# Six buffers instead of five for the splits of a Down phase, those splits ranked ahead of the weights' splits, and B22 loaded before B21

## The chip, the cores and the metric

One core of one Trainium2 chip runs the whole kernel. The metric is the device time of one execution in microseconds (us). The engines are named as the profile names them: PE (matmuls), PEld (its weight loads), ACT, DVE, POOL, and SP, which here issues nearly all DMAs.

## The reference, cut to what matters

```python
x = attention(q, k, v, omega)            # linear attention, 2304 tokens x 512
h = x @ w_in;  h = h * sigmoid(h)        # 512 -> 2048      "up 1"
x = h @ w_out                            # 2048 -> 512      "down 1"
g = x @ w_gate; v = x @ w_val            # 512 -> 1536      "up 2"
return (g * sigmoid(g) * v) @ w_out2     # 1536 -> 512      "down 2"
```

The weights come as float64 and are brought to float32 on the chip ("conv" in the code). All matrices are multiplied in float32 accuracy.

## The kernel before, in words

Five stages follow each other on PE: attention (0 to about 118 us), up 1 (to 292), down 1 (to 469), up 2 (to 722), down 2 (to the end).

Each matrix product of the four later stages is a Strassen scheme with seven products in place of eight, in the order `ORDER` = 1, 5, 6, 2, 7, 3, 4 (P1, P5, P6, P2, P7, P3, P4 below). Every product takes one block of the weights and one block of the tokens: B11 for P1, T1 = B12 - B11 for P5, T2 = B22 - T1 for P6, B21 for P2, T3 = B22 - B12 for P7, B22 for P3, T4 = B21 - T2 for P4. Each operand is split into a high part ("hi", a copy on ACT in the reduced format fp32r) and the rest ("lo", a subtraction on DVE), and three matmuls (hi hi, hi lo, lo hi) replace one.

A Down phase (`down_phase`) walks over three groups of 768 tokens (s = 0, 1, 2), in each over the seven products, and in each product over the pairs k of feature blocks: four pairs in down 1, three in down 2. One pair is 12 matmuls (line L1478). For each pair `split` makes the hi (ACT, L1337), the lo (DVE, L1341) and, in P1, P5, P6 and P2, one of T1 to T4 (DVE, L1361). Hi and lo take one buffer each from the free list `f_z`, and give both back when the pair's matmuls are done. The blocks B11, B12, B21, B22 come from DRAM (`zload`, L1311); B22 and B21 land in space that the weights of the up phase used until its last product. The weights of the Down phase are loaded (SP, L1282) and split (ACT L1286, DVE L1290) by `split_load`; three such groups belong to each product of down 1 (widths 768, 768, 512), two to each of down 2. The post-processing of a Down product is L1419 (ACT) and L1433 (DVE); that of an up product is L1120 and L1144 (ACT) and L1177 and L1161 (DVE).

What is put on which engine's queue, and when, is settled when the program is written, by a list scheduler: `streams` holds the waiting operations by kind ("z" the loads of the blocks, "wd" the weights of the Down phase, "split" the hi, lo and T operations, "x" the preparation of the next up phase, "conv" the conversion of weights). `flush` emits, ahead of each product, what would be ready by the scheduler's own clock; the earliest goes first, and of two that are close the stream that stands earlier in the table (0.1 us for each place). On the chip each engine then runs its queue in that fixed order. `hook1` is called ahead of every product of up 1 with the step n (24 steps) and the product p, and opens streams and buffers at fixed places: `open_z` takes two of the six weight buffers of the up phase and gives four of 768 columns to `f_z`. A fifth buffer `gap` of `f_z` lies between B21 and B22 and is given when the Down phase starts; it is taken away again for the last group of tokens, where the weights of up 2 are to be loaded over it.

Of the kernel before, what the change touches and what calls it, by code (L numbers as in the profile page):

```python
# [42 lines left out]
def kernel(  # L43
# [151 lines left out]
    class Stream:  # L195
# [31 lines left out]
    streams = {  # L227
        "z": Stream(0.2),
        "wd": Stream(1.0),
        "split": Stream(1.0),  # L230
        "x": Stream(1.2, DVE=3),
# [87 lines left out]
    W = {}  # L319

    def conv_job(kind, i, dram=None, side=False):
        b = {}
# [17 lines left out]
        def first(h):  # L340
            def go():
                b["c", h] = c = f_c.take()

                nc.scalar.activation(c, word(h, 1).bitcast(F32), AF.Prelu, scale=2.0**-112, alpha=-(2.0**32))  # L349

            return Op("ACT", cost("ACT", 512), go, ins=[key("r", h)], outs=[key("c", h)], slots=(f_c, 1))

# [967 lines left out]

    def down_phase(m, Wd, hook, gap_until=None):
        fp = FP[m]
        np_ = fp // 2
        K = lambda *k: ("d", m, *k)
        gap = cut(ra, 3072, 768)
        ops = {}
# [54 lines left out]
        yield st  # L1381
        f_z.give(gap)
        gone = []

# [71 lines left out]
        for s in range(NSB):  # L1456
            for p in ORDER:
                for k in range(np_):
# [28 lines left out]
                    for t in (hi, lo):  # L1487
                        n = len(lent)
                        lent[:] = [x for x in lent if x is not t]
                        if len(lent) < n:  # L1490
                            f_op.give(t)
                        elif t is not gap or (s, p) != gap_until and not gone:
                            f_z.give(t)
                        else:
                            gone.append(t)
                    if (s, p, k) == (*(gap_until or (0, 0)), np_ - 1) and not gone:
                        f_z.q = deque(x for x in f_z.q if x[0] is not gap)
                        gone.append(gap)
                    if s == NSB - 1 and (k == np_ - 1):
# [4 lines left out]
                ended(s, p)  # L1504
        f_z.q = deque((x, t) for x, t in f_z.q if x is not gap)

# [36 lines left out]
    Wd1, wd_ops = down_ops(0)  # L1543
    d1 = down_phase(0, Wd1, lambda *a: hook_d1(*a), (NSB - 1, 6))

# [3 lines left out]
    def open_z():  # L1549
# [4 lines left out]
        for i in range(4):  # L1554
            f_z.give(cut(ra, 7424 + i * 768, 768))

# [11 lines left out]
    def hook1(n, p):  # L1568
# [5 lines left out]
        if n == len(seq1) - 6 and p == 1:  # L1574
            streams["wd"].extend(wd_ops)
        if n == len(seq1) - 1 and p == 1:
            open_z()
# [7 lines left out]
    assert not to_come  # L1585
    streams["z"].extend(z_first(0, "B21", "B22"))

# [57 lines left out]
    while len(streams["conv"]):  # L1645
        assert drain()
    streams["z"].extend(z_first(1, "B21", "B22"))
    open_z()
# [50 lines left out]
```

## Time and profile before

| | |
|---|---|
| median of 3 runs | 852.97 us (851.78 to 855.28) |
| the profiled execution's own time | 853.52 us |
| its span in the trace | 851.7 us |
| granted PE clock, mean over the span | 0.998 of full |
| PE busy | 823.9 us of the span |

The profiled execution has 1.8 us outside its span, and stands 0.55 us above the median. PE's busy time counts the modelled end of a matmul: after a wait, the first matmul of a new run starts some 0.2 us later than the row's idle figure says, so losses below are counted from start to start. A matmul of a full run takes 0.162 us from start to start (24 of them span 4.06 us with the last one's end of 0.33 us), so a pair of 12 takes 1.94 us.

### The profile page before, as it was taken

Reading aid. Unit: us, or ns where it says so; the run is one execution under the profiler, and the core shown is the slowest. Engines: PE = TensorE matmul, PEld = TensorE weight load, DVE = VectorE, ACT = ScalarE, POOL = GpSimd, SP = SyncE. Lnnn points to the kernel's source line nnn. Section 1 sums busy time; section 2 is a strip of 40 time slices with the busy share of each in tenths; the row PEclk is TensorE's granted clock in tenths of the full one; section 3 lists DMA queues with packets and bytes.
Section 4 is the critical chain, followed back from the end, with each engine's and each line's share of the span. In section 5 each row is a group of like instructions: output and inputs, shape, how many; then the busy total and the mean of one; then the engine's idle time right before and its main releaser. Section 6 shows DMA issues by size and latency. Waiting matters only on the chain.

```text
span 851.7 us, 18196 instructions
## 1 busy us (share of the span) xinstructions
PE 823.9 (97%) x6889; PEld 796.4 (93%) x6889; DVE 623.8 (73%) x1016; ACT 552.5 (65%) x1166; POOL 164.8 (19%) x204
## 2 busy tenths in 40 slices
PE   8999999999999879999998998999999999999998
PEld 7888889999899879999998998999999999899998
DVE  4888877576644687796899998584757548979783
ACT  6999878776767854455557874655556557646552
POOL 0477831044440000000000035121213010000000
PEclk9999999999999999999999999999999999999999
DMA  8579866588999865608514657462637168483602
GB/s 284 183 259 299 282 211 226 173 260 282 333 310 364 286 231 165 206 22 243 181 62 141 218 179 208 146 204 100 211 97 238 53 212 283 169 272 94 220 3 75
DMA packets 110120, 170.09 MB, mean 200 GB/s; under 512 B 9424, under 2 KB 94032, under 8 KB 110032
## 3 DMA queue, kind: packets, MB, share of 16 engines
q1 hardware_dynamic: 109808, 168.69, 60.9%
q8 instruction: 54, 0.88, 0.4%
q14 instruction: 34, 0.28, 0.1%
q10 hardware_dynamic: 224, 0.23, 0.1%
HBM read 107.02 MB, written 61.87 MB: 198 GB/s over the span
## 4 chain that ended last, share of the span: by engine, by line
PE 76%; DVE 7%; DMA 7%; issue 4%; ACT 3%; POOL 2%; SPq 0%; DVEq 0%; ACTq 0%; POOLq 0%
PE ps L1103 36%; PE ps L1478 29%; PE ps L757 4%; PE ps L801 2%; PE ps L817 2%; DMA wd_out<-fa 2%; PE ps L848 2%; DMA ra<-g_d 2%; POOL fa L382 2%; DVE fa L363 1%; DMA fa<-in_moe_w_val 1%; DVE ra L1341 1%; DMA fa<-in_moe_w_out 1%; DVE ra L429 1%; PE ps L873 1%
## 5 line engine op out<-in xcount | busy, mean ns | idle before, releaser
L382 POOL TENSOR_TENSOR fa<-fa 128x256 f32<-128x256 f32 x124 | 105.6, 866 | 506.4 <-ACT fa L1144 239.3
L1103 PE MATMUL ps<-ra 128*128 128x384 f32 x840 | 148.4, 328 | 6.1 <-ACT ps L1120 4.0
L1103 PE MATMUL ps<-rb,ra 128*128 128x384 f32 x840 | 146.3, 327 | 2.1 <-ACT ps L1120 2.1
L1103 PE MATMUL ps<-rc,ra 128*128 128x384 f32 x840 | 145.8, 326 | 1.5 <-ACT ps L1120 1.5
L1103 PEld LDWEIGHTS ps<-ra 128*128 128x128 f32 x840 | 137.6, 189 | 9.0 <-ACT ps L1120 5.8
L1103 PEld LDWEIGHTS ps<-rb,ra 128*128 128x128 f32 x840 | 137.6, 189 | 3.6 <-ACT ps L1120 3.3
L1103 PEld LDWEIGHTS ps<-rc,ra 128*128 128x128 f32 x840 | 137.8, 189 | 2.5 <-ACT ps L1120 2.4
L1120 ACT ACTIVATE ps<-ps 128x384 f32<-128x384 f32 x180 | 85.4, 477 | 67.7 <-PE ps L1103 63.4
L1177 DVE TENSOR_TENSOR fa<-fa,ps 128x384 f32<-128x384 f32 x120 | 66.2, 551 | 80.5 <-ACT ps L1120 58.0
L1337 ACT ACTIVATE ra<-fa 128x768 fp32r<-128x768 f32 x86 | 71.9, 841 | 60.4 <-PE ps L1478 43.9
L1341 DVE TENSOR_TENSOR ra<-fa,ra 128x768 fp32r<-128x768 f32 x81 | 77.4, 955 | 21.6 <-PE ps L1478 13.4
L1478 PE MATMUL ps<-ra 128*128 128x384 f32 x486 | 84.0, 332 | 6.8 <-DVE ra L1341 5.7
L1478 PE MATMUL ps<-ra,rb 128*128 128x384 f32 x516 | 89.9, 327 | 0.4 <-DVE ra L1341 0.4
L1478 PEld LDWEIGHTS ps<-ra 128*128 128x128 f32 x486 | 80.7, 192 | 9.0 <-DVE ra L1341 7.4
L1478 PE MATMUL ps<-ra,rc 128*128 128x384 f32 x482 | 83.9, 327 | 2.2 <-DVE ra L1341 2.2
L1478 PEld LDWEIGHTS ps<-ra,rb 128*128 128x128 f32 x516 | 84.5, 189 | 1.4 <-DVE ra L1341 1.0
L773 ACT ACTIVATE kq<-ps,nb 128x128 f32<-128x128 f32 x288 | 79.3, 401 | 7.8 <-DVE nb L771 7.5
L1478 PEld LDWEIGHTS ps<-ra,rc 128*128 128x128 f32 x482 | 78.9, 189 | 3.4 <-DVE ra L1341 3.2
L349 ACT ACTIVATE fa<-fa 128x512 f32<-128x512 f32 x65 | 54.0, 833 | 20.2 <-DMA fa<-in_moe_w_in 5.7
L1361 DVE TENSOR_TENSOR fa<-ra,fa 128x768 f32<-128x768 f32 x63 | 60.0, 953 | 4.4 <-DMA ra<-g_d 3.7
L1144 ACT ACTIVATE fa<-fa 128x384 f32<-128x384 f32 x84 | 43.6, 519 | 25.5 <-DVE fa L1177 25.2
L363 DVE SCALAR_TENSOR_TENSOR fa<-fa 128x512 uint32<-128x512 uint32 x65 | 56.0, 862 | 0.7
(112 smaller groups left out, 1104.5 us busy)
## 6 DMA issues: line engine op xcount, KB each, us to landing
g_d<-fa SPq DMA_DIRECT2D x168, 192.0 KB, 4.1
fa<-g_d SPq DMA_DIRECT2D x42, 384.0 KB, 5.0
ra<-g_d SPq DMA_DIRECT2D x42, 384.0 KB, 4.3
fa<-in_moe_w_out SPq DMA_DIRECT2D x28, 512.0 KB, 5.1
fa<-in_moe_w_in SPq DMA_DIRECT2D x16, 512.0 KB, 5.0
wd_out<-fa SPq DMA_DIRECT2D x12, 512.0 KB, 3.2
fa<-in_moe_w_gate SPq DMA_DIRECT2D x12, 512.0 KB, 4.0
fa<-in_moe_w_val SPq DMA_DIRECT2D x12, 512.0 KB, 5.2
```

Of the source, the lines that this page charges most:

```text
L349: nc.scalar.activation(c, word(h, 1).bitcast(F32), AF.Prelu, scale=2.0**-112, alpha=-(2.0**32))
L363: nc.vector.scalar_tensor_tensor(c, word(h, 0), 29, c, op0=ALU.logical_shift_right, op1=ALU.bitwise_or)
L382: f(blk(f"S{n}"), blk(l), blk(r))
L773: nc.scalar.activation(e[:, g // 2, g % 2, h * M : (h + 1) * M], x[:, g, :], AF.Exp, bias=nb[:, g : g + 1])
L1103: nc.tensor.matmul(woven(ps[b][:, :N]), cut(l, j * P, P), halves(cut(r, j * N, N)), start=start and c == 0, stop=stop and c == 5, skip_gro ...
L1120: nc.scalar.activation(out() if callable(out) else out, src, AF.Copy)
L1144: nc.scalar.activation(b["t"], src, AF.Silu)
L1177: nc.vector.tensor_add(t, t if in_place else p5[n], ps[bank_][:, :N])
L1337: nc.scalar.activation(ops[s, p, k][0], src(), AF.Copy)
L1341: nc.vector.tensor_sub(l, src(), h.bitcast(F32))
L1361: (nc.gpsimd if eng == "POOL" else nc.vector).tensor_sub(z(PLACE[to]), z(PLACE.get(l, l)), z(PLACE.get(r, r)))
L1478: nc.tensor.matmul(woven(ps[BANKS[p] + e][:, :N]), cut(a, e * P, P), halves(b), start=p in FIRST and i == 0 and c == 0, stop=p in LAST and ...
```

## The change

Nothing is added to or taken from what is computed. The diff, with the parts that only count buffers left out:

```diff
     streams = {
         "z": Stream(0.2),
+        "split": Stream(1.0),
         "wd": Stream(1.0),
-        "split": Stream(1.0),
...
+    halved = []
...
         def first(h):
             def go():
                 b["c", h] = c = f_c.take()
+                halved[:] = [x for x in halved if x is not b] + ([b] if h == 0 else [])
...
-            return Op("ACT", cost("ACT", 512), go, ins=[key("r", h)], outs=[key("c", h)], slots=(f_c, 1))
+            return Op("ACT", cost("ACT", 512), go, ins=[key("r", h)], outs=[key("c", h)], slots=(f_c, 1), guard=lambda: h == 1 or not halved)
...
-        gap = cut(ra, 3072, 768)
+        spares = [cut(ra, 3072, 768), cut(ra, 6912, 768)]
...
-        f_z.give(gap)
-        gone = []
+        for t in spares:
+            f_z.give(t)
+        over = []
...
-                    if (s, p, k) == (*(gap_until or (0, 0)), np_ - 1) and not gone:
-                        f_z.q = deque(x for x in f_z.q if x[0] is not gap)
-                        gone.append(gap)
+                    for t, x in zip(spares, until or ()):
+                        if (s, p, k) == (*x, 0):
+                            over.append(t)
+                            f_z.q = deque(y for y in f_z.q if y[0] is not t)
...
-    d1 = down_phase(0, Wd1, lambda *a: hook_d1(*a), (NSB - 1, 6))
+    d1 = down_phase(0, Wd1, lambda *a: hook_d1(*a), ((NSB - 1, 2), (NSB - 1, 3)))
...
-            f_z.give(cut(ra, 7424 + i * 768, 768))
+            f_z.give(cut(ra, 7680 + i * 768, 768))
...
-        if n == len(seq1) - 1 and p == 1:
+        if n == len(seq1) - 2 and p == 5:
             open_z()
...
-    streams["z"].extend(z_first(0, "B21", "B22"))
+    streams["z"].extend(z_first(0, "B22", "B21"))
...
-    streams["z"].extend(z_first(1, "B21", "B22"))
+    streams["z"].extend(z_first(1, "B22", "B21"))
```

In the changed program the lines of interest stand three further down: L1337, L1341, L1361 are L1340, L1344, L1364; L1286, L1290, L1282 are L1289, L1293, L1285; L1311 is L1314, L1177 is L1180, L1129 is L1132, L586 is L589, L1433 is L1440. PE's matmuls come in the same order as before, but for the buffers that they read. POOL's queue is the same.

**DVE at the start of down 1.** `fa<-fa,ps` is the last post-processing of up 1, `rb<-rb` and `rc<-rc` are lo parts of weights, `ra<-fa,ra` is a pair's lo, `fa<-fa` is T1 and `fa<-ra,fa` is T2 or T3. Before:

```order
L1177 TENSOR_TENSOR fa<-fa,ps_83 128x384
L1290 TENSOR_TENSOR rb<-rb 128x768
L1341 TENSOR_TENSOR ra<-fa,ra 128x768
L1361 TENSOR_TENSOR fa<-fa 128x768
...
L1290 TENSOR_TENSOR rc<-rc 128x512
L1341 TENSOR_TENSOR ra<-fa,ra 128x768
L1290 TENSOR_TENSOR rc<-rc 128x768 x2
L1361 TENSOR_TENSOR fa<-fa 128x768
L1341 TENSOR_TENSOR ra<-fa,ra 128x768
L1361 TENSOR_TENSOR fa<-ra,fa 128x768
```

Now, from the second-last step of up 1 on:

```order
L1344 TENSOR_TENSOR ra<-fa,ra 128x768
L1364 TENSOR_TENSOR fa<-fa 128x768
L1344 TENSOR_TENSOR ra<-fa,ra 128x768
L1180 TENSOR_TENSOR fa<-fa,ps_80 128x384
L1364 TENSOR_TENSOR fa<-fa 128x768
...
L1180 TENSOR_TENSOR fa<-fa,ps_83 128x384
L1293 TENSOR_TENSOR rb<-rb 128x768
L1344 TENSOR_TENSOR ra<-fa,ra 128x768
L1364 TENSOR_TENSOR fa<-fa 128x768
L1344 TENSOR_TENSOR ra<-fa,ra 128x768
L1364 TENSOR_TENSOR fa<-fa 128x768
L1344 TENSOR_TENSOR ra<-fa,ra 128x768
```

Lo and T1 of P1's first two pairs have moved ahead of up 1's end, and the splits of `rc`, of which seven stood between P1's third pair and P6's second, now start after P7's second pair; one split of `rb` stands in P6.

**SP at the same place.** `ra<-g_d` are the loads of B21 and B22, `rc<-wd_out` the weights, `g_d<-fa` the last stores of up 1. Before:

```order
L1129 DMA g_d_64<-fa 128x384 x8
L1282 DMA rc<-wd_out 128x512
L1282 DMA rc<-wd_out 128x768 x2
L1129 DMA g_d_64<-fa 128x384 x2
L1311 DMA ra<-g_d_64 128x2x384 x8
L1282 DMA rc<-wd_out 128x512
```

Now:

```order
L1132 DMA g_d_64<-fa 128x384 x7
L1314 DMA ra<-g_d_64 128x2x384 x6
L1132 DMA g_d_64<-fa 128x384 x2
L1314 DMA ra<-g_d_64 128x2x384
L1132 DMA g_d_64<-fa 128x384
L1314 DMA ra<-g_d_64 128x2x384
L1285 DMA rc<-wd_out 128x512
L1285 DMA rc<-wd_out 128x768 x2
```

The first four of the eight loads were B21 and are now B22; they have passed three loads of weights and three stores.

**ACT at the end of down 1.** `ra<-fa 128x768` are the hi parts of P4's pairs, `ra<-ra 128x448` the hi parts of up 2's first weights (gate four, then val four), 128x384 the preparation of up 2's tokens. Before:

```order
L1337 ACTIVATE ra<-fa 128x768
L586 ACTIVATE rb<-fa 128x384
L1286 ACTIVATE ra<-ra 128x448
L1337 ACTIVATE ra<-fa 128x768
L1286 ACTIVATE ra<-ra 128x448 x4
L1337 ACTIVATE ra<-fa 128x768
```

Now:

```order
L1289 ACTIVATE ra<-ra 128x448 x2
L1340 ACTIVATE ra<-fa 128x768
L1289 ACTIVATE ra<-ra 128x448 x2
L1340 ACTIVATE ra<-fa 128x768
L1289 ACTIVATE ra<-ra 128x448 x4
L589 ACTIVATE rb<-ra 128x384
L1340 ACTIVATE ra<-fa 128x768
```

Each fence ends with the hi of P4's fourth pair: all eight splits of weights now stand before it (five before), and one of tokens.

**DVE in down 2, where P7's weights are split.** `fa<-ra,fa` closes P2, the lo parts after it are P7's three pairs and P3's first two. Now:

```order
L1364 TENSOR_TENSOR fa<-ra,fa 128x768
L1344 TENSOR_TENSOR ra<-fa,ra 128x768
L1344 TENSOR_TENSOR rb<-fa,rb 128x768 x2
L1344 TENSOR_TENSOR ra<-ra 128x768 x2
L1293 TENSOR_TENSOR rb<-rb 128x768
```

Before, the lo of P7's first weights (`rb<-rb`) stood ahead of P5's first pair:

```order
L1161 TENSOR_TENSOR fa<-fa 128x384
L1290 TENSOR_TENSOR rb<-rb 128x768
L1290 TENSOR_TENSOR rc<-rc 128x768 x2
L1341 TENSOR_TENSOR ra<-fa,ra 128x768
L1361 TENSOR_TENSOR fa<-ra,fa 128x768
```

It has moved behind the lo parts of fourteen pairs: three each of P5, P6, P2 and P7, and two of P3.

## Rows read from the trace of the kernel before

**Rows 1.** Page: the span, and the granted clock in 40 slices.

```profile
span 851.7 us, 18196 instructions
...
PEclk9999999999999999999999999999999999999999
```

**Rows 2.** Waits of PE over the whole span: us in total, times, longest.

```profile
PE ps L1478 <- DVE ra L1341: 8.3, 10, 2.0
```

**Rows 3.** Busy time by stretch: us, PE, PEld, DVE, ACT, POOL, clock, DMA share, GB/s.

```profile
290.00:320.00 30.00, 23.41 (x123) 21.25 (x123) 26.04 (x32) 17.95 (x28) 0.00 (x0) 0.94 0.62 209
320.00:430.00 110.00, 110.00 (x679) 110.00 (x678) 87.73 (x99) 56.75 (x79) 0.00 (x0) 1.00 0.53 158
```

**Rows 4.** Timeline of PE from 276 to 325 us: start, us, what [idle before, releaser].

```profile
275.70 14.63 PE L1103 MATMUL ps<-rc,ra 128*128 128x384 f32 x89
290.80 1.24 PE L1103 MATMUL ps<-rc,ra 128*128 128x384 f32 x6 [0.47 <-ACT ps L1120]
293.33 0.43 PE L1478 MATMUL ps<-ra 128*128 128x384 f32 x1 [1.12 <-ACT ra L1337]
294.33 6.12 PE L1478 MATMUL ps<-ra 128*128 128x384 f32 x36 [0.56 <-DVE ra L1341]
300.65 2.22 PE L1478 MATMUL ps<-ra 128*128 128x384 f32 x12 [0.21 <-DVE ra L1341]
304.13 2.22 PE L1478 MATMUL ps<-ra 128*128 128x384 f32 x12 [1.26 <-DVE ra L1341]
308.33 9.89 PE L1478 MATMUL ps<-ra 128*128 128x384 f32 x48 [1.98 <-DVE ra L1341]
319.21 1.08 PE L1478 MATMUL ps<-ra 128*128 128x384 f32 x5 [0.98 <-DVE ra L1341]
```

**Rows 5.** Busy time by stretch of 4 us, columns as in rows 3.

```profile
306.00:310.00 4.00, 2.02 (x12) 1.72 (x11) 3.52 (x4) 0.84 (x1) 0.00 (x0) 0.96 1.05 389
310.00:314.00 4.00, 4.00 (x16) 4.00 (x16) 3.52 (x5) 2.83 (x4) 0.00 (x0) 0.61 0.21 78
```

**Rows 6.** Timeline of DVE and SP's issues from 284 to 325 us.

```profile
289.66 0.96 DVE L1290 TENSOR_TENSOR rb<-rb 128x768 fp32r<-128x768 f32 x1 [2.40 <-ACT rb L1286]
...
292.33 1.35 SPq L1282 DMA_DIRECT2D rc<-wd_out  x3
...
294.68 6.46 SPq L1311 DMA_DIRECT2D ra<-g_d  x8
...
300.52 1.82 DVE L1290 TENSOR_TENSOR rc<-rc 128x768 fp32r<-128x768 f32 x2
...
306.45 0.96 DVE L1361 TENSOR_TENSOR fa<-ra,fa 128x768 f32<-128x768 f32 x1 [2.37 <-DMA ra<-g_d]
307.32 0.95 DVE L1341 TENSOR_TENSOR ra<-fa,ra 128x768 fp32r<-128x768 f32 x1
...
317.60 0.68 DVE L1290 TENSOR_TENSOR rc<-rc 128x512 fp32r<-128x512 f32 x1
```

**Rows 7.** Timeline of PE and ACT near the end of down 1.

```profile
454.60 8.22 PE L1478 MATMUL ps<-ra,rc 128*128 128x384 f32 x48 [1.53 <-DVE ra L1341]
...
463.34 6.04 PE L1478 MATMUL ps<-ra,rc 128*128 128x384 f32 x35 [0.52 <-DVE ra L1341]
...
463.50 1.97 ACT L1286 ACTIVATE ra<-ra 128x448 fp32r<-128x448 f32 x4
465.43 0.84 ACT L1337 ACTIVATE ra<-fa 128x768 fp32r<-128x768 f32 x1
```

**Rows 8.** Timeline of PE at the start of down 2.

```profile
722.22 2.11 PE L1478 MATMUL ps<-ra 128*128 128x384 f32 x12
...
731.04 4.00 PE L1478 MATMUL ps<-ra 128*128 128x384 f32 x23 [0.69 <-DVE ra L1341]
...
735.63 0.43 PE L1478 MATMUL ps<-rb 128*128 128x384 f32 x1 [0.42 <-DVE rb L1341]
...
738.24 2.22 PE L1478 MATMUL ps<-rb 128*128 128x384 f32 x12 [0.39 <-DVE rb L1341]
...
740.84 0.43 PE L1478 MATMUL ps<-ra,rb 128*128 128x384 f32 x1 [0.39 <-DVE ra L1341]
```

More of the change, by code (lines that the diff above doesn't have):

```diff
@@ L1319, in zload, with down_phase @@
         )
-    def down_phase(m, Wd, hook, gap_until=None):
+    def down_phase(m, Wd, hook, until=None):
         fp = FP[m]
@@ L1381, in down_phase, with closed_z @@
         yield st
-        f_z.give(gap)
-        gone = []
+        for t in spares:
+            f_z.give(t)
+        over = []
+        def closed_z(t):
+            return any(t is x for x in over)
         def out_(s, c, e, t, key):
@@ L1491, in down_phase @@
                             f_op.give(t)
-                        elif t is not gap or (s, p) != gap_until and not gone:
+                        elif not closed_z(t):
                             f_z.give(t)
-                        else:
-                            gone.append(t)
-                    if (s, p, k) == (*(gap_until or (0, 0)), np_ - 1) and not gone:
-                        f_z.q = deque(x for x in f_z.q if x[0] is not gap)
-                        gone.append(gap)
+                    for t, x in zip(spares, until or ()):
+                        if (s, p, k) == (*x, 0):
+                            over.append(t)
+                            f_z.q = deque(y for y in f_z.q if y[0] is not t)
                     if s == NSB - 1 and (k == np_ - 1):
@@ L1504, in down_phase @@
                 ended(s, p)
-        f_z.q = deque((x, t) for x, t in f_z.q if x is not gap)
+        f_z.q = deque((x, t) for x, t in f_z.q if not any(x is y for y in spares))
     def up_order(kinds, n, head, tail):
```

## The prediction

> **What bounds the kernel now.** The page comes first: PE's granted clock is at the 2.4 GHz level in all forty slices [rows 1], so what can be won is time in which PE waits. The waits of PE over the span name the largest cause: a Down phase's matmuls wait 8.3 us for lo parts [rows 2]. The table by stage shows where. In the middle of down 1 PE is busy 110.00 of 110 us, while in the 30 us at its start it is busy 23.4, with DVE busy 26.0 [rows 3]. So five buffers lose nothing once the phase runs, and the loss lies at the seams.
>
> The timeline of PE at the first seam is read from start to start [rows 4]. The last product of up 1 starts at 290.80; 89 matmuls from 275.70 end at 275.70 + 89 x 0.162 = 290.12, so 0.7 us is lost ahead of it. Its six matmuls, and a single one that only waits for weights, end at about 292.05. From there to 319.21 PE does 108 matmuls of down 1 (P1 and P5 with 48 each, P6's first pair with 12), which at 0.162 us are 17.5 us. It takes 27.2. **The seam costs 9.7 us and the 0.7 ahead of it: 10.4 us.**
>
> In parts: P1's first matmul waits for its hi, and the second for its lo (1.3 and 0.8). P1's fourth pair comes 0.5 late, P5's first 1.5, P5's second 2.3, P6's second 3.1. Three causes stand behind these. DVE makes seven splits of weights that PE does not need before P7 (three of 0.68 and four of 0.91, 5.5 us in all; one row has a pair of the long ones, one is the last short one [rows 6]). T2 of P5's first pair waits 2.37 us with DVE idle, for B22, the fifth of eight loads issued from 294.68 on, which came behind three loads of weights and two stores; P5's second lo, one instruction later on DVE's queue, starts only at 307.32 [rows 6]. And after these waits (PE busy 2.02 of 4 us) the granted clock falls to 0.61 over four us, that is, part of them at the 1.2 GHz level [rows 5]: the 48 matmuls from 308.33 take 9.9 us where 48 x 0.162 and the end of 0.2 are 7.9, so 1.9 of the 3.1 is clock.
>
> **The change, part by part.** No instruction is added or removed on any engine, so every term is a wait that goes or comes.
>
> *Start of down 1.* Two hi (0.84 us each [rows 7]), two lo (0.95) and two T1 (0.96 [rows 6]) go into the last two steps of up 1. There ACT has five times 0.5 us of L1120 and L1144 and some weights in each step of 6.8, and DVE stands idle up to 2.40 us at a time [rows 6]. If that cover fails, a hi ahead of an L1120 that PE waits for costs at most its 0.84; I take 0.2. I then walk the new queues with the durations of the rows, from the last product's end at about 291.8. P1's first two pairs are ready, so PE starts at once. The buffers of the third pair lie partly over the last product's weights, so its hi starts at 291.8; hi and lo are done at 293.7, and PE wants them at 295.7. From then on the hi of a pair may start when the pair three before it is done, 3.9 us ahead of need; hi and lo take 1.8, so about 2 us is left for what DVE does between them. That is one T (0.96) in each pair and one split of rb (0.91) in P6. The seven splits of rc now stand beside P7's and P3's pairs, where DVE has no T: 0.95 of each 1.94 us is taken there, so twelve pairs leave 12 us for 5.5.
>
> B22 needs the space that the last product frees at 291.8 and is then first on SP. Eight loads took 6.46 us to issue and moved at 389 GB/s when the queue was full [rows 5, 6], that is 1.0 us for 384 KB. I take B22's first part to land at 296 to 300 (the upper end by the delay of 8 us that the loads had before, behind three more). T2 must start by 299.5 for P5's second lo to be ready in time, so at worst 0.5 is lost. With the waits gone PE does not stand half idle, and the clock stays up. Left over: 0.2 in up 1, 0.4 here. **Gain 10.4 - 0.6 = 9.8**; bounds 5 (rivals below) and 10.4.
>
> *The sixth buffer.* Three whole pairs instead of two and a half, of which only two could be in use. In the steady part it is worth nothing [rows 3]. At the seam it is what makes the 2 us of slack: with two pairs the hi could start only 1.94 us ahead, hi and lo take 1.8, and each T that falls between is late. The Trainium skill (Trainium Kernel Development and Optimization, Best Practices) asks for double buffering and names no gain from a third set. The stretch from 320 to 430 us agrees with it: two sets, no wait [rows 3]. By that rule the third pair is worth nothing at the seam either; that is a rival below.
>
> *End of down 1, start of up 2.* Losses before: P3's second pair starts at 454.60 and its 48 matmuls end at 462.4, P4's second starts at 463.34 [rows 7], 1.0 late. DVE stands there behind the adds of the product before, and that stays. New is that ACT does all eight splits of up 2's weights and one of tokens before the hi of P4's fourth pair. Walked through: DVE has two more splits of 0.55 ahead of P4's second lo and one token operation less, so the pair starts 0.6 later. Then four L1286 of 0.49 and one of tokens (0.45, estimated from these by width) stand between the hi of the third and that of the fourth pair: 464.0 + 5 x 0.48 + 0.84 + 0.95 = 468.2, where PE wants it at 464.0 + 3.9 = 467.9, so 0.3. In up 2's first step two token splits stand ahead of the copy that P6 waits for, and three ahead of the one that P7 waits for; each must first be subtracted on DVE. I make that 0.6 and 0.4. Cost 1.9; the first conversion's ACT and DVE parts stand earlier in up 2's queues, which may return 0.4. **Cost 1.5**, bounds 0 (all hidden) and 3.5 (val's load late, so that ACT stands before it). The earlier retirement of the two spare buffers adds nothing that I can find: from P7 on two pairs are in use, as before.
>
> *Start of down 2.* Here ten and more buffers were free before. The starts give the lateness [rows 8]. The phase starts at 722.22; four pairs and one matmul, 49, end 49 x 0.162 later, at 730.2, and the next starts at 731.04. From there 24 matmuls end at 731.04 + 3.89 = 734.9, and the next starts at 735.63; twelve more end 1.94 later, at 737.6, and the next starts at 738.24; the same again, 740.2 and 740.84. In all 0.8 + 0.7 + 0.6 + 0.7 = 2.8 us, the first from T2 waiting for B22, the others from splits of weights between the lo parts. B22 first and the weights later remove these. In return the split of P7's first weights stands behind the lo of P3's second pair. Without waits each of the phase's products of 36 matmuls takes 5.83: P2 is the fourth and its second pair ends at 722.2 + 3 x 5.83 + 3.9 = 743.6, which frees the buffers of that hi. With hi and lo of 1.8 its lo ends at 745.4 and the split at 746.4, while PE wants P7 at 722.2 + 4 x 5.83 = 745.5. **Gain 2.8 - 0.9 = 1.9**, bounds 0.5 and 2.6.
>
> *Sum.* 9.8 - 1.5 + 1.9 = 10.2. The profiled execution took 853.5 (the table of times), which gives 843.3; it stands 0.55 above the median, so **842.8 us**.
>
> The order of the conversions (the guard on L349) leaves POOL's queue as it was; I put it at nothing, hidden behind up 2's matmuls.
>
> **The rivals.**
> 1. *The weights' splits only move.* DVE was busy 26 of 30 us at the seam [rows 3], so it could be DVE's sum that binds, and the 5.5 us come back as waits of P7 to P4: 848.3. For it: that busy share. Against it: the 12 us of room, and 87.7 of 110 us in the next stretch [rows 3].
> 2. *B22 is late all the same.* If it lands at 305 whatever its place, because the last product holds its space, some 5 us stay: 847.8. Against it: before, its issue came at the earliest at 294.68 and fifth.
> 3. *The third pair brings nothing*, two being enough for PE to work on one while the other is made: then P1's third and P5's first three pairs are each late by about 0.5 us (1.8 + 0.96 for hi, lo and T, less the 1.94 that a pair gives, part of it caught up): 2 us, 844.8. For it: the steady part, where two suffice [rows 3]; against it: T, which that part has too, but with its loads there in time. This is how it comes out by the Trainium skill's page named above.
> 4. *The end of down 1 costs its upper bound*: val's load took the time up to ACT's reach, and up 2's first step waits at each copy, 2 us more: 844.8.
> 5. *Slower than before.* DVE runs in order and its adds (L1433) wait for a product's end. With lo parts emitted further ahead, an add may now stand before a lo that PE needs; before, this cost 1.8 us at 454.60 (a wait of 1.53 by the row, and some 0.3 for the restart as at the other waits [rows 7]). There are two such places in each group of tokens, twelve in all. If six of them cost 1.8 the gain is gone; all twelve give 864. Against it: in the new queues lo parts of three pairs stand ahead of most of these adds.
>
> **How the numbers follow.** Forecast 0.60, rivals 1 to 5: 0.10, 0.07, 0.10, 0.10, 0.03. A change of 0.5% is 4.3 us, about what a measurement of this kernel can tell from none, so the border of faster is 848.7. The forecast, rivals 2 to 4 and half of rival 1 lie below it: faster 0.90, same 0.07, slower 0.03. The range starts at 840.0, with the seam at 10.4, nothing paid at the end of down 1 and 2.6 won in down 2 (853.0 - 13.0), and ends at 847.8, which takes in rivals 2 to 4.
>
> **What the changed profile would show.** Right: in the 30 us at the start of down 1 PE is busy over 29 with the clock at 1.00 throughout; T2 (L1364) waits for no DMA; P6's second pair starts about 17.5 us after up 1's last product. At the end of down 1 there are waits of PE for a lo of P4's second and fourth pair, then waits of up 2's first step for copies of L1123, 2 to 3 us in all. In down 2 one wait remains, P7's first pair for weights (L1293), of 0.5 to 1 us. Wrong: waits of down 1's P7 or P3 for L1293 on rc (rival 1), a DMA ahead of T2 (rival 2), waits of P1's third or P5's pairs for lo (rival 3), a clock below 0.9 anywhere after 120 us, or waits for L1344 that end just after an L1440 in the first two groups of tokens (rival 5).

## The result

The changed kernel takes **841.18 us** (median of five, 840.23 to 842.80) against 852.97 us, a ratio of 0.9862 with an interval of 0.9841 to 0.9883: 11.8 us less. The forecast was 842.8 us, in a range of 840.0 to 847.8. The profiled execution took 842.80 us, with a span of 841.0 us; it is the slowest of the five.

The page of the changed kernel, as in [rows 1]:

```profile
span 841.0 us, 18097 instructions
PEclk9999999999999999999999999999999999999999
```

The busy instructions of each engine are as many as before (PE 6889, DVE 1016, ACT 1166, POOL 204 on both pages); the 99 that the span has fewer are not among them.

Its waits of PE over the whole span, in us, times, longest; the 8.3 us of [rows 2] are 1.4 (line numbers are up to seven higher than before: L1340 is the hi, L1344 the lo, L1364 T, L1289 and L1293 the weights' splits, L1123 the first part of an up product's post-processing, L1426 and L1440 a Down product's):

```profile
PE ps L1106 <- ACT ps L1123: 10.3, 13, 1.7
...
PE ps L1485 <- DVE ra L1344: 1.4, 2, 1.1
...
PE ps L1485 <- DVE rb L1293: 0.5, 1, 0.5
```

Its busy time in the two stretches of [rows 3], with the same columns:

```profile
290.00:320.00 30.00, 30.00 (x187) 30.00 (x186) 28.27 (x33) 22.75 (x37) 0.00 (x0) 1.00 0.68 235
320.00:430.00 110.00, 110.00 (x679) 110.00 (x678) 92.81 (x107) 57.65 (x83) 0.00 (x0) 1.00 0.51 154
```

PE, busy 23.41 of the 30 us before, is now busy 30.00 of 30, at a clock of 1.00 where it was 0.94. In the first stretch DVE does more than before, 28.27 us against 26.04, and PE does not wait for it. The mean granted clock of all five executions is 1.000, where it was 0.998 in the profiled one before.

The timeline of PE at the places of [rows 4], [rows 7] and [rows 8]:

```profile
273.92 19.66 PE L1106 MATMUL ps<-rc,ra 128*128 128x384 f32 x120
293.42 0.34 PE L1413 MATMUL ps<-ra 128*128 128x384 f32 x1
293.60 18.69 PE L1485 MATMUL ps<-ra 128*128 128x384 f32 x114
312.12 18.20 PE L1485 MATMUL ps<-ra,rb 128*128 128x384 f32 x111
...
444.34 8.22 PE L1485 MATMUL ps<-ra,rc 128*128 128x384 f32 x48 [0.27 <-DVE ra L1344]
453.68 6.04 PE L1485 MATMUL ps<-ra,rc 128*128 128x384 f32 x35 [1.12 <-DVE ra L1344]
...
462.08 2.22 PE L1106 MATMUL ps<-ra 128*128 128x384 f32 x12 [0.41 <-ACT ps L1123]
464.58 1.24 PE L1106 MATMUL ps<-rb,ra 128*128 128x384 f32 x6 [0.28 <-ACT ps L1123]
...
496.94 1.24 PE L1106 MATMUL ps<-ra 128*128 128x384 f32 x6 [1.46 <-ACT ps L1123]
...
738.09 1.89 PE L1485 MATMUL ps<-ra,rb 128*128 128x384 f32 x10 [0.52 <-DVE rb L1293]
```

At the first seam there is not one wait: the last product of up 1, a matmul that only waits for weights, and down 1 follow each other without a gap. Waits are left at the end of down 1 (444.34 and 453.68), in the first steps of up 2, and one at P7's first pair in down 2.

Since single executions differ by more than some of the effects below, the experiments are read by stage too. A stage lasts from its first matmul to that of the next one in the timeline of PE; each row is one profiled execution, in us.

| kernel | attention | up 1 | down 1 | up 2 | down 2 | median |
|---|---|---|---|---|---|---|
| before | 118.1 | 175.2 | 175.9 | 253.0 | 129.5 | 853.0 |
| changed | 119.6 | 174.0 | 166.0 | 254.1 | 127.3 | 841.2 |
| e1 B21 first | 117.9 | 172.9 | 166.2 | 254.6 | 128.0 | 840.7 |
| e2 weights first | 117.9 | 174.1 | 173.7 | 252.0 | 128.2 | 847.5 |
| e3 five buffers | 118.2 | 173.1 | 168.7 | 252.8 | 126.5 | 841.4 |
| e4 given back earlier | 119.6 | 174.1 | 168.0 | 252.7 | 127.4 | 842.6 |
| e5 loads ahead | 119.2 | 173.9 | 170.7 | 254.5 | 127.4 | 845.4 |
| e6 loads behind | 118.1 | 173.3 | 171.1 | 251.8 | 128.3 | 846.0 |
| e7 rank only | 120.1 | 174.5 | 168.9 | 252.7 | 126.7 | 843.4 |
| e8 B22 only | 118.9 | 175.5 | 173.3 | 252.7 | 128.2 | 850.1 |
| e9 buffers only | 118.6 | 174.8 | 178.4 | 251.9 | 129.8 | 853.3 |
| e10 six, then five | 118.9 | 173.0 | 166.0 | 253.8 | 126.5 | 839.7 |
| e11 as e10, conv later | 118.0 | 174.3 | 166.0 | 256.7 | 126.6 | 843.4 |
| e12 as e10, conv latest | 118.3 | 173.2 | 166.0 | 258.5 | 126.5 | 844.4 |

The attention stage has the same instructions in all of these and takes 117.9 to 120.1 us; so a difference of 1 us in one profiled total says nothing. Up 1 also moves by about 1 us between kernels that have the same order there. The changed kernel's profiled execution lost 1.5 us in attention against that of before, and won 12.2 in the other four stages.

### The profile page after: what moved, and what is told of

Same layout as the page of the kernel before. It is cut to its first block, busy times and chain, and to the rows that moved or that the text cites. A ratio compares the mean times of both kernels' runs of the same rounds, so it can differ in the third digit from the quotient of the medians.

```text
span 841.0 us, 18097 instructions
## 1 busy us (share of the span) xinstructions
PE 819.3 (97%) x6889; PEld 795.4 (95%) x6889; DVE 623.3 (74%) x1016; ACT 549.0 (65%) x1166; POOL 167.3 (20%) x204
## 4 chain that ended last, share of the span: by engine, by line
PE 77%; DMA 7%; DVE 5%; ACT 5%; issue 3%; POOL 2%; SPq 0%; ACTq 0%; DVEq 0%; POOLq 0%
PE ps L1106 35%; PE ps L1485 32%; PE ps L760 4%; PE ps L804 2%; DMA fa<-in_moe_w_out 2%; PE ps L820 2%; PE ps L851 2%; POOL fa L385 2%; DMA wd_out<-fa 2%; ACT kq L776 2%; DMA g_d<-fa 1%; DVE fa L366 1%; ACT ps L1123 1%; ACT fa L1147 1%; DVE ra L432 1%
## 5 line engine op out<-in xcount | busy, mean ns | idle before, releaser
L385 POOL TENSOR_TENSOR fa<-fa 128x256 f32<-128x256 f32 x124 | 107.8, 884 | 494.0 <-DVE fa L366 283.3
L1106 PE MATMUL ps<-ra 128*128 128x384 f32 x840 | 148.3, 328 | 7.0 <-ACT ps L1123 6.4
L1123 ACT ACTIVATE ps<-ps 128x384 f32<-128x384 f32 x180 | 85.1, 476 | 66.7 <-PE ps L1106 62.9
L1180 DVE TENSOR_TENSOR fa<-fa,ps 128x384 f32<-128x384 f32 x120 | 66.3, 552 | 81.6 <-ACT ps L1123 58.6
L1340 ACT ACTIVATE ra<-fa 128x768 fp32r<-128x768 f32 x87 | 73.1, 843 | 63.4 <-PE ps L1485 57.3
L1344 DVE TENSOR_TENSOR ra<-fa,ra 128x768 fp32r<-128x768 f32 x87 | 83.1, 957 | 20.2 <-ACT ra L1340 18.1
L1485 PE MATMUL ps<-ra,rb 128*128 128x384 f32 x528 | 87.5, 326 | 0.5 <-DVE rb L1293 0.5
L1485 PE MATMUL ps<-ra,rc 128*128 128x384 f32 x486 | 80.9, 327 | 1.4 <-DVE ra L1344 1.4
L1485 PE MATMUL ps<-ra 128*128 128x384 f32 x486 | 80.3, 326 | 0.0
L1364 DVE TENSOR_TENSOR fa<-ra,fa 128x768 f32<-128x768 f32 x63 | 60.1, 954 | 0.7
```

What stands on the lines that cost most here:

```text
L385: f(blk(f"S{n}"), blk(l), blk(r))
L1106: nc.tensor.matmul(woven(ps[b][:, :N]), cut(l, j * P, P), halves(cut(r, j * N, N)), start=start and c == 0, stop=stop and c == 5, skip_gro ...
L1123: nc.scalar.activation(out() if callable(out) else out, src, AF.Copy)
L1180: nc.vector.tensor_add(t, t if in_place else p5[n], ps[bank_][:, :N])
L1340: nc.scalar.activation(ops[s, p, k][0], src(), AF.Copy)
L1344: nc.vector.tensor_sub(l, src(), h.bitcast(F32))
```

## The experiments

Each was run beside the kernel before on the same chip, in five rounds, and the ratio in brackets, with its interval, is against that. There were three batches on three chips (e1 to e4, e5 to e8, e9 to e12), in which the kernel before took 853.04, 853.40 and 852.82 us; medians of different batches are compared with that much of doubt.

**e1, B21 first again** (0.9847, 0.9828 to 0.9866). In the changed kernel, for both phases:

```diff
-    streams["z"].extend(z_first(0, "B22", "B21"))
+    streams["z"].extend(z_first(0, "B21", "B22"))
```

> The changed kernel (841.2 us) with B21 loaded ahead of B22 again, in both Down phases. Theory A (three causes together, the sixth buffer gives 2 us of slack): B22's first part is issued four loads later, about 2 to 3 us, so T2 of P5's first pair waits about 2 us at 300 us, of which the slack hides most; 0.5 to 1 us lost at the start of down 1, and the 0.8 us of T2's wait in down 2 comes back: 842.2 to 843. Theory B (B22's place alone made the gain at the seam): its wait of 2.4, the clock's 1.9 and the 0.8 come back: 846 or more. Theory C (B22 is late or early whatever its place): 841.2, with no wait of T2 for a load.

Measured 840.67 us (839.29 to 841.46), no slower than the changed kernel. On DVE the first T2 waits, and nothing behind it is late:

```profile
299.04 0.96 DVE L1364 TENSOR_TENSOR fa<-ra,fa 128x768 f32<-128x768 f32 x1 [1.42 <-DMA ra<-g_d]
```

The timeline of PE shows no wait between up 1's last product and 441 us; from start to start the first 114 matmuls of down 1 take 0.3 us more than in the changed kernel. So with the rest of the change in place the order of B21 and B22 gives nothing that the medians show. Theory B falls; A's 0.5 to 1 us at the seam did not come either. Down 2 is 0.7 us longer, near the 0.8 that A had; about half of it lies where T2 waits for B22 (1.60 us on DVE).

**e2, weights ranked first again** (0.9930, 0.9912 to 0.9949):

```diff
-        "split": Stream(1.0),
         "wd": Stream(1.0),
+        "split": Stream(1.0),
```

> The changed kernel with the weights' splits ranked ahead of the blocks' splits, as in the kernel before; six buffers and B22 first stay. On DVE six splits of rc (5 us) stand again among the pairs of P1 and P5. Theory A: 2 us of slack hide a part, 3 to 4 us are lost at the start of down 1, PE waits there for lo parts, and 1 to 2 us come back at the start of down 2, less a 0.5 us for the weights of P7 there: 845 to 847. Rival 1 (DVE's sum binds, the order only moves the waits): 841.2 within 1 us.

Measured 847.47 us (845.97 to 849.07): 6.3 of the 11.8 us are gone again. Down 1 is 7.7 us longer (173.7 against 166.0) and up 2 2.1 shorter. Rival 1 falls: with the same work on DVE, the order in which it is queued costs this much or nothing. But the rows held something that theory A does not say. SP's issues, DVE, PE, and the busy time by stretch in e2:

```profile
294.64 2.24 SPq L1285 DMA_DIRECT2D rc<-wd_out  x3
296.93 6.92 SPq L1314 DMA_DIRECT2D ra<-g_d  x8
```

```profile
304.61 0.96 DVE L1364 TENSOR_TENSOR fa<-ra,fa 128x768 f32<-128x768 f32 x1 [2.42 <-DMA ra<-g_d]
```

```profile
306.49 11.90 PE L1485 MATMUL ps<-ra 128*128 128x384 f32 x53 [3.77 <-DVE ra L1344]
```

```profile
304.00:308.00 4.00, 1.51 (x5) 1.51 (x6) 3.39 (x5) 1.08 (x2) 0.00 (x0) 0.70 1.06 373
308.00:312.00 4.00, 4.00 (x13) 3.62 (x12) 3.97 (x5) 0.84 (x1) 0.00 (x0) 0.50 0.67 238
```

B22 is the first block here, and T2 waits 2.42 us for it all the same, as in [rows 6] where it was the fifth (2.37). The rank that puts the weights' splits ahead puts their *loads* ahead too, six of them, and the blocks' loads begin only at 296.93. In the changed kernel it is the other way round on SP:

```profile
291.76 3.77 SPq L1314 DMA_DIRECT2D ra<-g_d  x6
...
299.92 4.56 SPq L1285 DMA_DIRECT2D rc<-wd_out  x7
```

During PE's wait of 3.77 us the granted clock falls (0.70 over those four us), and it stands at 0.50, the 1.2 GHz level, for the next four. So there were two ways in which the rank could act, through SP's queue (theory S) and through the queues of the engines that split (theory D, which names DVE alone), and e5 and e6 were made to separate them.

**e3, five buffers** (0.9862, 0.9843 to 0.9881). The second spare is left out, and with it its place in the list of returns:

```diff
-        spares = [cut(ra, 3072, 768), cut(ra, 6912, 768)]
+        spares = [cut(ra, 3072, 768)]
```

> The changed kernel with five buffers: the second spare (the one at column 6912) is left out, the early opening, the ranks and B22 first stay. Theory A: two pairs in use give no slack for what DVE does between hi and lo; the splits of rb and rc that stand beside P6's and P2's T cost about 0.7 us each, four of them, and the start of P1's third pair 0.2: 843.5 to 845, lost between 294 and 330 us. Rival 3 (the third pair brings nothing, two sets being enough): 841.2 within 1 us.

Measured 841.35 us (841.01 to 843.59): the sixth buffer gives nothing that can be measured. The stages show a trade under that. PE in e3:

```profile
309.85 7.26 PE L1485 MATMUL ps<-ra,rb 128*128 128x384 f32 x43
317.29 8.25 PE L1485 MATMUL ps<-ra,rb 128*128 128x384 f32 x48 [0.18 <-DVE ra L1344]
325.71 4.01 PE L1485 MATMUL ps<-ra,rb 128*128 128x384 f32 x23 [0.18 <-DVE ra L1344]
...
445.47 8.22 PE L1485 MATMUL ps<-ra,rc 128*128 128x384 f32 x48 [1.53 <-DVE ra L1344]
```

The 114 matmuls from 309.85 (in P6, P2 and P7) take 19.7 us from start to start, where 114 x 0.1625 = 18.5 are needed and the changed kernel takes no more. So e3 loses 1.2 us there, at the second pairs of P2 and P7, and nothing in P1 and P5; the 2 us that I had given the third pair are not reached. The larger loss, 1.6 us of the 2.8 by which down 1 is longer, is at the *end* of down 1: the wait of 1.53 before P3's second pair is there as in [rows 7], where the changed kernel waits 0.27. ACT shows why, in e3 and, from 440.19, in the changed kernel:

```profile
441.86 0.84 ACT L1340 ACTIVATE ra<-ra 128x768 fp32r<-128x768 f32 x1
...
443.02 0.84 ACT L1426 ACTIVATE ps<-ps 128x384 f32<-128x384 f32 x2
```

```profile
440.19 0.82 ACT L1340 ACTIVATE ra<-ra 128x768 fp32r<-128x768 f32 x1
441.51 0.96 ACT L1426 ACTIVATE ps<-ps 128x384 f32<-128x384 f32 x2 [0.50 <-PE ps L1485]
```

The hi of P3's second pair stands ahead of P7's L1426 on ACT's queue. By the diff e3 has four buffers at this place and the changed kernel five: of its spares one goes back at P2's first pair, the other at P3's. With four, all are held by P7's last pair and P3's first, and the hi starts only when P7's matmuls are done; L1426 follows a token copy later, DVE's adds wait for L1426, and the pair's lo stands behind the adds. With a fifth buffer the hi is done before P7 ends, and L1426 waits for nothing but P7's matmuls. What the sixth buffer gives in down 1, 2.8 us of stage, is taken back in up 2 (1.3) and down 2 (0.8); the rest is below what the medians tell.

**e4, the spares given back earlier** (0.9872, 0.9854 to 0.9890). The order of products is P1, P5, P6, P2, P7, P3, P4, so P6 comes *before* P2, and the two buffers are taken away earlier here than in the changed kernel. The expectation is muddled on this; its theories hold all the same.

```diff
-    d1 = down_phase(0, Wd1, lambda *a: hook_d1(*a), ((NSB - 1, 2), (NSB - 1, 3)))
+    d1 = down_phase(0, Wd1, lambda *a: hook_d1(*a), ((NSB - 1, 6), (NSB - 1, 6)))
```

> The changed kernel, but in the last group of tokens of down 1 both spare buffers are kept until P6's first pair, where the kernel before kept its one until P6's end (they go at the first pairs of P2 and P3 in the changed one, P6 being before these in the order of products... that is, they go earlier here only if the program's order counts them so). The transfers of the next stage's tokens into that space move with it. By my step that the place where they are given back adds nothing: 841.2 within 1 us, with the end of down 1 and up 2 as they are. Rival: the end of down 1 gained and up 2 lost by it; then those move by 1 us or more against each other (up 2's 254.1 us nearer the 253.0 of the kernel before).

Measured 842.62 us (842.08 to 843.44). PE waits longer again at P3's second pair:

```profile
447.06 8.22 PE L1485 MATMUL ps<-ra,rc 128*128 128x384 f32 x48 [1.76 <-DVE ra L1344]
```

Down 1 is 2.0 us longer and up 2 1.5 shorter than in the changed kernel. So it is the late return that saves the wait at P3, and that costs up 2: in e4, as in the kernel before, up 2's first step has no wait, while in the changed kernel it has two (462.08 and 464.58 above). With the weights ranked first (e2, e6, e9) a late return does not lengthen up 2, which takes 251.8 to 252.0 us there. Gain and cost nearly cancel: by stages 0.6 us is left, by medians 1.4 with intervals that overlap.

**e5, the weights' loads ahead** (0.9907, 0.9878 to 0.9936). The changed kernel with six loads emitted before the blocks'; the added time only keeps the scheduler from moving the splits too:

```diff
+    for o in list(streams["wd"].q["SP"])[:6]:
+        if o.ready() is not None:
+            streams["wd"].emit(o)
+            T[o.outs[0]] += 10.0
     streams["z"].extend(z_first(0, "B22", "B21"))
```

> The changed kernel (841.2 us), with six loads of weights for P7 and P3 (rc) put ahead of the loads of B22 and B21 on SP's queue, where ranking the weights first had put them; on DVE the splits keep the order of the changed kernel but for one (rb), which moves ahead of P5's first T2. Theory S (the rank works through SP: the weights' loads delay B22): the loads of B22 start about 5 us later, T2 waits 3 to 4 us for B22, PE's fifth pair is late by about as much and the clock falls after it: 845 to 848. Theory D (the rank works through DVE: weights' splits ahead of lo parts): 841 to 842.

Measured 845.38 us; the single times lie further apart than any other kernel's, 841.88 to 850.68. SP's issues, DVE and PE:

```profile
291.24 3.08 SPq L1285 DMA_DIRECT2D rc<-wd_out  x6
...
296.54 6.91 SPq L1314 DMA_DIRECT2D ra<-g_d  x8
```

```profile
304.10 0.96 DVE L1364 TENSOR_TENSOR fa<-ra,fa 128x768 f32<-128x768 f32 x1 [4.22 <-DMA ra<-g_d]
```

```profile
305.99 10.56 PE L1485 MATMUL ps<-ra 128*128 128x384 f32 x53 [2.83 <-DVE ra L1344]
```

T2 waits 4.22 us for B22 with DVE's splits of rc still behind the lo parts. Three stores stand between the six loads and the blocks', so that these come after both. Down 1 is 4.8 us longer in this execution, which is 2.1 us above the median; the 53 matmuls from 305.99 take 10.56 us in place of 8.8, so 1.8 of the 4.8 is clock. Theory S holds: the place of the loads is worth this without the splits on DVE, but for the one of rb that the expectation names.

**e6, the loads behind** (0.9912, 0.9891 to 0.9934). The kernel of e2, with a guard on the loads of the weights of P7, P3 and P4:

```diff
+                guard=lambda: m == 1 or p not in (7, 3, 4) or ("z", 0, 0, "B21", 3) in T,
```

> The kernel of the second experiment (weights ranked first, 847.5 us), but the loads of the weights of P7, P3 and P4 wait until those of B22 and B21 are issued. DVE's splits of weights still come ahead of lo parts, in groups of three or four of 2.5 to 3.4 us in P6 and P2. Theory S: T2 waits for no load, PE waits little at the start of down 1 (under 1.5 us in all), the clock stays up: 841 to 843.5. Theory D: about as slow as with the loads ahead, 845 to 848, with waits of PE for lo parts in P6 and P2.

Measured 846.01 us (844.47 to 846.79). SP's issues, ACT, DVE, PE and the busy time by stretch (lines up to one higher than in the changed kernel):

```profile
289.42 4.50 SPq L1315 DMA_DIRECT2D ra<-g_d  x7
...
300.00 4.67 SPq L1286 DMA_DIRECT2D rc<-wd_out  x7
```

```profile
309.44 4.08 ACT L1290 ACTIVATE rc<-rc 128x512 fp32r<-128x512 f32 x6
```

```profile
315.15 3.03 DVE L1294 TENSOR_TENSOR rc<-rc 128x512 fp32r<-128x512 f32 x4
318.10 0.95 DVE L1365 TENSOR_TENSOR fa<-ra,fa 128x768 f32<-128x768 f32 x1
```

```profile
314.30 0.43 PE L1486 MATMUL ps<-ra,rb 128*128 128x384 f32 x1 [1.27 <-ACT ra L1341]
...
319.97 13.76 PE L1486 MATMUL ps<-ra,rb 128*128 128x384 f32 x83 [2.46 <-DVE ra L1345]
```

```profile
318.00:322.00 4.00, 2.03 (x12) 2.03 (x13) 4.00 (x6) 0.98 (x3) 0.00 (x0) 1.00 0.05 8
322.00:326.00 4.00, 4.00 (x27) 4.00 (x26) 4.00 (x6) 1.69 (x2) 0.00 (x0) 1.00 0.69 201
```

The blocks' loads come first, no T2 waits for one, and PE still waits 2.46 us for a lo: four splits of weights, 3.03 us, and a T stand ahead of it. Down 1 is 5.1 us longer than in the changed kernel. So theory D holds, but not for DVE alone: before that PE waits 1.27 us for a *hi*, because six hi parts of weights, 4.08 us, stand ahead of it on ACT, and then for its lo. From start to start 2.3 us are lost there and 2.7 at 319.97. Each of the two theories alone costs about 5 us of down 1, both together, in e2, 7.7; by the medians it is 4.2, 4.8 and 6.3.

**e7, the rank alone** (0.9880, 0.9858 to 0.9902): the kernel before with only the two lines of the table exchanged.

> The kernel before (853.0 us) with the blocks' splits ranked ahead of the weights', and nothing else: five buffers, opened late, B21 first. If the rank is the whole change (B21 or B22 first and the sixth buffer made no difference by the runs so far): 841 to 843. My prediction's sum, in which the rank, B22 and the sixth buffer each take part: 845 to 848. Rival: the fifth buffer's late opening makes P1's first pairs late, and 1 to 2 us more.

Measured 843.39 us (842.77 to 844.57), 0.4 us above the first expectation's range and 1.6 us below the range that my sum gave. SP issues seven of the blocks' loads from 292.02 on, with no load of weights ahead of them, and no T2 waits although B22 comes second:

```profile
292.02 3.89 SPq L1311 DMA_DIRECT2D ra<-g_d  x7
```

One line of the change makes 9.6 of its 11.8 us (10.0 against the 853.40 of its own batch). What it lacks in down 1, some 3 us, lies where e3 loses it: 1.2 us in P2 and P7, and the wait of 1.53 us at P3's second pair. Up 2 and down 2 are 2.1 us shorter than in the changed kernel.

**e8, B22 first alone** (0.9957, 0.9943 to 0.9972): the kernel before with the two `z_first` lines changed.

> The kernel before with B22 loaded ahead of B21, and nothing else. By my prediction's reading (T2's wait of 2.4 us comes from B22 standing behind B21): about 2.4 and the clock's 1.9 less at the start of down 1, and up to 0.8 in down 2: 848 to 850. Theory S (B22 is late because weights' loads and stores stand ahead of all the blocks' loads): at most four issues earlier, 1 to 3 us of B22's lateness: 850 to 853.

Measured 850.05 us (849.52 to 850.85), at the border of the two expectations: 2.9 us less (3.4 against its own batch), 2.6 of it in down 1. T2 waits for no load, but PE still waits for lo parts behind splits of weights (1.05, 0.64 and 0.99 us). The clock falls here too, only earlier: it is 0.58 over the four us from 294, in P1, and the 48 matmuls from 295.43 take 9.34 us in place of 8.0. B22's place is worth something only where its loads are late.

**e9, the buffers alone** (1.0008, 0.9999 to 1.0017): the changed kernel with the rank of e2 and the loads of e1.

> The kernel before (853.0 us) with the sixth buffer, the early opening and the later return of the spares, but weights ranked first and B21 loaded first. If the rank is what matters and the buffers nothing by themselves: the start of down 1 as long as before (down 1 173 to 177 us), 850 to 854. By my prediction's step (the sixth buffer gives 2 us of slack): 848 to 850, with fewer waits of P5's pairs.

Measured 853.32 us (852.26 to 855.41), the time of the kernel before. DVE and PE:

```profile
310.64 0.96 DVE L1364 TENSOR_TENSOR fa<-ra,fa 128x768 f32<-128x768 f32 x1 [5.86 <-DMA ra<-g_d]
```

```profile
312.52 6.07 PE L1485 MATMUL ps<-ra 128*128 128x384 f32 x24 [8.37 <-DVE ra L1344]
```

Six loads of weights stand ahead of B21 and B22 here (three in the kernel before), T2 waits 5.86 us and PE 8.37. More buffers don't help where the load is late.

**e10, six buffers in down 1 and five in down 2** (0.9849, 0.9836 to 0.9862):

```diff
-        spares = [cut(ra, 3072, 768), cut(ra, 6912, 768)]
+        spares = [cut(ra, 3072, 768), cut(ra, 6912, 768)][: 2 - m]
```

> The changed kernel with six buffers in down 1 and five in down 2. The kernels with five buffers so far had a down 2 of 126.5 to 126.7 us, those with six 127.3; P7's wait for its first weights (0.5 us) should go, since with five buffers the blocks' splits run less far ahead of the weights'. So down 2 about 126.6 us, and 840.5; rival: the 0.5 us come from elsewhere, down 2 stays at 127.3 and the time at 841.2.

Measured 839.68 us (839.27 to 840.61). Down 2 is 126.5 us, as expected, and P7 waits for no weights. It has the lowest median of all, but its interval overlaps that of the changed kernel, so only the 0.8 us of the stage is shown.

**e11 and e12, the conversions in up 2 later** (0.9893, 0.9878 to 0.9908, and 0.9904, 0.9890 to 0.9917). As e10, with

```diff
-            streams["conv"].ahead = 0.8
+            streams["conv"].ahead = 0.4
```

and 0.2 in e12.

> As the last, and the conversion of weights in up 2 is emitted up to 0.4 us ahead of the scheduler's time in place of 0.8. My reading of up 2 (254.1 us where matmuls alone would take some 248): its waits come from conversions that stand ahead of L1123 on ACT. If so up 2 shortens by 1 to 3 us: 838 to 840. Rival: the conversions themselves are due by then, and later ones make products wait for weights (L432): 841 or more.

> As the last with 0.2 us. If conversions ahead of L1123 are the cause, a little more of up 2's waits goes: 837.5 to 840. If conversions are due: waits for L432 grow and it is slower than the last by 1 us or more.

Measured 843.35 (842.06 to 845.91) and 844.44 us (843.86 to 845.15), slower than e10 by 3.7 and 4.8. My reading is half right. From up 2's start to about 540 us the waits for L1123 fell from 5.3 us (in the changed kernel and in e10) to 2.0 and 1.8, but one wait for converted weights took their place, 4.17 us in e11 and 6.80 in e12, and the clock fell with it. PE and the busy time in e11:

```profile
503.16 1.65 PE L1106 MATMUL ps<-ra 128*128 128x384 f32 x4 [4.17 <-DVE ra L432]
```

```profile
504.00:508.00 4.00, 4.00 (x14) 4.00 (x13) 3.93 (x9) 1.36 (x3) 1.73 (x2) 0.50 0.58 178
```

All of PE's waits in up 2 sum to 6.5 us in e11, 5.8 in e10; so of the 2.9 us by which up 2 is longer some 2.2 are left for the clock, which is 0.50 here and 1.00 in e10. The conversions are due by then; they can't simply be put later.

## Why the prediction was right, and where its steps were not

**Start of down 1: right in size, half right in cause.** I gave it 9.8 of the 10.4 us lost there [rows 4]; all of it is gone. That DVE's sum binds (rival 1) was wrong, as DVE's 28.27 of 30 us without a wait shows. Of the three causes that I named, the splits of weights on DVE hold (e6). The second was misread. [Rows 6] show three loads of weights and two stores ahead of the blocks' loads, and I counted them, but credited the cure to "B22 needs the space that the last product frees and is then first on SP". It is the rank that makes the blocks' loads first on SP (e5, e7); with the rank, B22 may come second and nothing is lost (e1). The change of rank therefore takes away both causes at once, and the third, the clock, with them. The first was also named for DVE alone: e6 shows the weights' hi parts on ACT in the way of a pair's hi as well. And [rows 1] was misread: a slice's 9 stands for 90% or more, so the clock that falls in [rows 5] does not show in it.

**The sixth buffer: wrong step.** "At the seam it is what makes the 2 us of slack": with five buffers the seam loses 1.2 us (e3), in P2 and P7. My walk let each T that falls between hi and lo make the lo late; in e7, which has five buffers too, lo and T follow each other on DVE every 1.95 us, and PE waits for none of them before 320 us. Rival 3 had its mechanism in part and its price of 2 us too high, and not where it put it, at P1 and P5. The Trainium skill (Trainium Kernel Development and Optimization, Best Practices) asks for double buffering, to overlap DMA with compute, and names no gain from a third set. The medians agree with it, 841.35 against 841.18 us (e3); the stages show a gain in down 1 and losses behind it. The larger part of the gain is at another place than I looked, the end of down 1.

**End of down 1 and start of up 2: mis-sized by 2.0 us.** I forecast 1.5 us of cost. 84 pairs of 12 matmuls at (312.12 - 293.60)/114 = 0.1625 us take 163.8 us. Down 1 lost 12.1 us above that before, 8.3 of them from 293.33 to 319.21 [rows 4], so 3.8 at its end; now it loses 2.2 in all. So the end gained 1.6 us, and up 2 lost 1.1: 0.5 us of gain in place of 1.5 of cost. The step that failed is "DVE stands there behind the adds of the product before, and that stays". At P4's second pair it stayed and grew as forecast, from 0.52 to 1.12 us (0.6 forecast). But at P3's second pair the wait of 1.53 fell to 0.27, from start to start 1.4 us less, by the extra buffer and its late return (e3, e4). And P7's fourth pair, which I had not listed, was 0.9 us late in the kernel before (its 114 matmuls from 429.32 would end at 447.8) and is not late now:

```profile
429.32 19.26 PE L1478 MATMUL ps<-ra,rb 128*128 128x384 f32 x114
...
448.90 4.17 PE L1478 MATMUL ps<-ra,rc 128*128 128x384 f32 x24 [0.15 <-DVE ra L1341]
```

I also had the return itself the wrong way round: it is later, not earlier, than before. The 0.3 us at P4's fourth pair did not come. The first step of up 2 was right: I had 0.6 and 0.4 us for its two copies, and from start to start they are 0.58 and 0.55 late (462.08 and 464.58, idle 0.41 and 0.28). That is all of the 1.1 us; the 0.4 that might return did not, for the other waits of up 2 sum to 5.1 us before and after. They stand elsewhere: the wait of 1.46 us for L1123 at 496.94 is in place of 0.89 and 0.42 us for splits of tokens that PE waited for some 4 us earlier in the stage before the change.

**Start of down 2: right.** 2.2 us shorter, where 1.9 was forecast, with the single wait at P7's first weights as described (0.52 us of idle time, 0.7 from start to start; 0.9 forecast).

**The sum.** The three terms measured 10.4 + 0.5 + 2.2 = 13.1 us, where 9.8 - 1.5 + 1.9 = 10.2 were forecast; 2.0 of the difference is the second seam. The stages show 12.2, since other waits within up 1 took 0.9 us more in this execution; e1, with the same instructions there, has an up 1 that is 1.1 us shorter. That 842.8 came within 1.6 us of the median is therefore partly luck: the terms were 2.9 us too small. Two small sums of the prediction are off without moving it: the seven splits are 5.7 us, not 5.5, and the chances that it adds up for faster make 0.92, not 0.90. Rival 5 did not come: PE does not wait once between 273.92 and 444.34. POOL's queue is the same before and after, but no run takes the guard on L349 out alone, so that it costs and gives nothing is not shown.

**Left open:** why e5's single times spread over 9 us. The mean granted clock is 1.000 in its fastest execution (841.88 us), 0.996 in the slowest (850.68) and 0.997 or 0.998 in the four between, so the clock takes part; it is not shown that it is all. Beside the rank, the sixth buffer gives 2.8 us in down 1 and costs 2.1 behind it by the stages; the early opening, B22 first and the guard together give nothing from down 1 on (548.0 us in e3, 548.3 in e7). The medians fall by 2.7 us from e7 to e1, which are of two batches, with intervals that overlap a little, while the stages from down 1 on sum to 0.6 us more; so what is left beside the rank is not settled to better than that.

## What to carry to other kernels

A rank in a scheduler moves everything that a stream issues, its loads too: when work is moved ahead, look first at which transfers it puts ahead of which on the issuing queue, for there six loads that nobody needed yet cost as much as the misplaced splits. Two causes of one wait don't add: each alone costs about 5 us of down 1 here (e5, e6) and both together 7.7 (e2), so taking one of two away shows only 2.6 or 2.9. Only experiments that undo each part alone in the finished kernel, and add each alone to the first one, show which line carries the gain. A buffer more can pay where a queue that is worked off in order has an instruction that needs a buffer ahead of one that others wait for, and the place may be far from the one it was made for; read the stages behind it too, for here they took most of it back (e3).

## What was not expected of the hardware

The granted clock does not follow from the waiting alone, as far as these rows show. In the kernel before, four us with PE busy 2.02 were followed by four at 0.61 [rows 5]. In e6's profile, PE is busy 2.03 of 4 us, after two stretches that were not full either, and the clock stays at 1.00 through the next four. In e2, after 1.51 of 4, it stood at 0.50. The clearest pair is e8 and the kernel before, with nearly the same waits at the start of P1. In e8, busy time by stretch:

```profile
290.00:294.00 4.00, 2.84 (x16) 2.23 (x14) 2.94 (x4) 3.24 (x6) 0.00 (x0) 1.00 0.19 68
294.00:298.00 4.00, 3.09 (x9) 2.76 (x10) 3.38 (x4) 2.85 (x5) 0.00 (x0) 0.58 0.95 176
```

In the kernel before:

```profile
290.00:294.00 4.00, 2.17 (x10) 1.32 (x9) 3.29 (x5) 3.24 (x7) 0.00 (x0) 1.00 0.37 128
294.00:298.00 4.00, 3.67 (x22) 3.66 (x23) 3.79 (x5) 2.34 (x4) 0.00 (x0) 1.00 0.89 196
```

PE waits 1.12 us for P1's first hi in both, and the clock falls in one and not in the other. Nor is it a matter of the kernel: of e6's five executions the profiled one, the fastest, has a mean clock of 1.000, the other four 0.996 to 0.998. So about the same waiting cost 1.9 us of clock in one execution and none in another; what decides it is not shown here.
